# Sums of taps in four tiles of 32 tokens instead of two of 64, all four in one PSUM tile of four banks

## The chip, the cores and the metric

The kernel runs on one core of one Trainium2 chip. A core has five engines with a queue of instructions each: TensorE (PE, matrix products, with its weight loads shown apart as PEld), VectorE (DVE), ScalarE (ACT), GpSimd (POOL) and SyncE (SP). They meet through semaphores. TensorE writes its products to PSUM, a memory of 128 partitions by eight banks of 512 fp32 values each. Nothing else here writes it, and ACT copies its content to SBUF. The metric is the time of one execution on the device, in microseconds (us), and lower is better.

## The reference: a dynamic convolution and a maxout layer

The first half takes `x` (8 batches, 4160 tokens, 192 features) and `weight_gen` (8 heads, 7 taps for each token):

```python
w = np.exp(weight_gen - max); w = w / (np.sum(w, axis=-1, keepdims=True) + 1e-09)
x_pad = np.concatenate([zeros(B, 6, D), x], axis=1)
out = np.einsum('bshk,bskhg->bshg', w, x_unf)   # x_unf: seven neighbouring tokens
```

So each token becomes a weighted sum of itself and the six tokens before it, with weights of its own for each of 8 heads of 24 features. The second half is applied to each of the 33280 tokens:

```python
h1 = x @ w1; h2 = x @ w2          # 192 -> 1024
g = np.maximum(h1, h2)
out = g @ w_out                   # 1024 -> 192
```

## The kernel before: tiling, stages and the order of work

Tokens lie on 128 partitions, 260 consecutive ones ("columns") on each. The columns are worked through in batches of 16 and in units of 4 columns (the first eight units, which make up the first two batches) or 8 columns (the others).

For each unit DVE multiplies `x` by the weights, all seven taps at once, into `m_t` (`mul`, L192); the weights come from ACT (`en_t`, L177). The seven taps are then added and the result is transposed, so that features lie on partitions, as the products that follow need it. In the later units DVE does the additions (`adds`, L208 to L217) and a DMA transposes. In units 0 to 7 TensorE does both (`sum_transpose`, L249): it loads a piece of `m_t` as weights and multiplies by the identity, and the taps add up in PSUM. Before the change a piece is 64 partitions by 128 columns of `m_t`, and 64 columns of the identity move through it. For each of 6 pieces and each tap there are two such matmuls, one on either half of the partitions, that write two different banks: 84 in a unit (48 in unit 5, where four taps are left after an addition on DVE). ACT then copies the sum to `yt` (L265).

The maxout is written as `w_out` applied to `h1 + relu(h2 - h1)`. The difference of the two weights is `wd`, and `hid_tile` (L309) multiplies `yt` by it. ACT's relu (L319) brings the product to SBUF as `rd_t`. The part of `h1` is one product with `w10`, the product of `w1` and `w_out`, computed once at the start: `w1_transposed` (L617), ACT's copies to `w1t` (L689), `w10_product` (L671) and `w10_copies` (L680, L682). Results are collected in PSUM as `op_ps`: `out_first` writes the `w10` part (L361) and one half of the hidden features (L349), and `out_second` the other half. Between these two ACT passes a signal on (`relay`, L382), since the halves meet in one bank. ACT's `evac` (L405) copies the results to `o_t`, and SyncE stores them.

The order of instructions of each engine is that of the Python code (`manual_schedule`). The code of the start stands out line by line. After it, `hidden(g, ...)` (L470) issues one group of tiles at a time: all hidden tiles of the group but the last, `out_first`, relus, the last hidden tile, its relu, `out_second`, `evac`, and then whatever the table `early` adds for that group. Groups 4 to 7 have two hidden tiles each, and `early` puts `sum_transpose(4)` to `sum_transpose(7)` behind their `evac`. From group 8 on there are three tiles and `later_ps` has divided PSUM anew; units of 8 columns come through DVE and the DMA from there.

PSUM in the first stage has two pools of two buffers of two banks each. Pool "h" holds hidden products. Pool "o" holds, by turns, the sums of `sum_transpose` (`yps`), the transposed `w1` (`tp`), the product `pw` and the results `op_ps`. A new tile waits until the reader of the tile before the last is done with that buffer.

Of the kernel before, what the change touches and what calls it, by code (L numbers as in the profile page):

```python
# [9 lines left out]
FP32 = mybir.dt.float32  # L10
BF16 = mybir.dt.bfloat16
# [6 lines left out]
def _sub(base: bass.AP, off: int, dims):  # L18
    ap = [list(base.ap[0])] + [[int(s), int(c)] for s, c in dims]
    return dataclasses.replace(base, offset=base.offset + off, ap=ap)  # L20
# [3 lines left out]
def kernel(  # L24
# [9 lines left out]
    nc = tc.nc  # L34
# [4 lines left out]
    P = 128  # L39
# [25 lines left out]
    for b, (c0, n) in enumerate(BATCHES):  # L65
# [19 lines left out]
    pyt = work.enter_context(tc.tile_pool(name="pyt", bufs=6))  # L85
    prd = work.enter_context(tc.tile_pool(name="prd", bufs=7))
    first_ps = work.enter_context(ExitStack())
    ps = {k: first_ps.enter_context(tc.tile_pool(name="pps_" + k, bufs=2, space=bass.MemoryType.PSUM))
          for k in ("h", "o")}

    def later_ps():

# [8 lines left out]
    m_t = pm.tile([P, K * 16 * D], BF16, name="m_t")  # L101
# [141 lines left out]
    def half(j):  # L243
        return slice(64 * j, 64 * j + 64)
# [4 lines left out]
    def sum_transpose(u, taps=range(K)):  # L249

        b, o, n = UNITS[u]
        assert n == 4
        yps = ps["r" if "r" in ps else "o"].tile([P, 1024], FP32, name="yps", tag="op")
        for k in range(6):
            for t in taps:
                for r in range(2):
                    at = (K * o + t * n) * D + k * P
                    nc.tensor.matmul(  # L258
                        yps[:, r * 512 + k * 64:r * 512 + (k + 1) * 64],
                        lhsT=m_t[half(r), at:at + P], rhs=ident[half(r), half(r)],  # L260
                        start=(k == 0 and t == taps[0]), stop=(t == taps[-1]),
                        skip_group_check=True,
                    )
        yt = pyt.tile([P, 8 // 2 * 3 * P], BF16, name="yt", tag="yt")
        yt_of[u] = nc.scalar.copy(out=_sub(yt, 0, [[64, 2], [P, 6], [1, 64]]),  # L265
                                  in_=_sub(yps, 0, [[512, 2], [64, 6], [1, 64]]))
        yt_ts[u] = yt


    relu_of, yt_of, w10_of = {}, {}, []  # L270
# [168 lines left out]
    for g in range(3, len(GROUPS)):  # L439
        most = 4 if g == 3 else 2 if GROUPS[g][1] == 2 or len(OUTS[-1]) == 4 else 4  # L440
        n = min(most, ready[g] - c)
# [21 lines left out]
    def out_room(now, tag=None):  # L463
        tag = tag or ("r" if "r" in ps else "o")
        w, name = {"ab": (2048, "ab"), "c": (1024, "c")}.get(tag, (1024, "op"))
        tile_ = ps[tag].tile([P, w], FP32, name="op_ps", tag=name)
        for c in now:
            op_at[c // 2] = tile_, (c - now[0]) // 2 * D

    def hidden(g, now=(), between=lambda: None, beside=lambda: None, ahead=lambda: None):  # L470


        t0, n = GROUPS[g]
        rd = room(g)
        for t in range(t0, t0 + n - 1):
            hid_tile(t)
        if now:
            out_room(now, "ab" if n == 1 and "ab" in ps else None)
            last = out_first(now)
        if len(now) > 2:  # L480
            relu(rd, t0, n - 1)
        else:
            for t in range(t0, t0 + n - 1):
                relu(rd, t, 1)
        if now:
            go = relay(last)
        hid_tile(t0 + n - 1)
        if len(now) > 2:
            beside()
        relu(rd, t0 + n - 1, 1)  # L490
        ahead()
        if now:
            out_second(now, go)
            evac(now[0] // 2, len(now) // 2)
        between()
        if len(now) <= 2:
            beside()

    def rest_of_results(c):

        parts = [p for p in (c[:4], c[4:-2], c[-2:]) if p]
        assert max(map(len, parts)) <= 4
        go = []
        for i, now in enumerate(parts):
            out_room(now, ("r", "ab", "c")[i])
            go.append(relay(out_first(now)))
            if i:
                out_second(parts[i - 1], go[i - 1])
                evac(parts[i - 1][0] // 2, len(parts[i - 1]) // 2)
        out_second(parts[-1], go[-1])  # L510
        evac(parts[-1][0] // 2, len(parts[-1]) // 2)
# [6 lines left out]
    ident = consts.tile([P, P], BF16, name="ident")  # L518
# [9 lines left out]
    with tc.tile_pool(name="pstage", bufs=1) as pstage:  # L528
# [7 lines left out]
        for p0, p1 in ((1, 16), (16, P)):  # L536
            nc.sync.dma_start(  # L537
                out=xs[p0:p1, 0:PAD * D],
                in_=bass.AP(tensor=x.tensor, offset=(p0 * CPP - PAD) * D,
                            ap=[[CPP * D, p1 - p0], [1, PAD * D]]),  # L540
# [20 lines left out]
        for wi, wsrc in enumerate((moe_w1, moe_w2)):  # L561
            for h in range(2):
                nc.sync.dma_start(  # L563
                    out=ws["T", wi][half(h), :],
                    in_=bass.AP(tensor=wsrc.tensor, offset=P * F + h * HF, ap=[[F, 64], [1, HF]]),
# [20 lines left out]
        for o in (0, 4, 8, 12):  # L586
            weights(0, o)
        nc.vector.tensor_copy(out=xb_ts[0][:, PAD * D:(PAD + 4) * D],
                              in_=xs[:, PAD * D:(PAD + 4) * D])
# [19 lines left out]

        def w1_transposed():  # L610

            tp = ps["o"].tile([P, 1024], FP32, name="tp", tag="op")[:, :].bitcast(BF16)
            for at, kind, nr in ((0, "E", P), (P, "T", 64)):
                for fi in range(FCH):
                    o = fi // 4 * 1024 + fi % 4 * D
                    rows, c = (slice(0, P), fi) if kind == "E" else (half(fi // 4), fi % 4)
                    nc.tensor.matmul(  # L617
                        tp[:, o + at:o + at + nr],
                        lhsT=w1[kind][rows, c * P:(c + 1) * P],
                        rhs=ident[rows, rows], is_transpose=True, skip_group_check=True,  # L620
                    )
            return tp
# [3 lines left out]
        def keep_warm(times):  # L626
# [11 lines left out]
            out=wo[:, :].rearrange("p (f d) -> p f d", d=D),  # L638
            in_=bass.AP(tensor=moe_w_out.tensor, offset=0, ap=[[D, P], [P * D, FCH], [1, D]]),
        )  # L640

        sum_transpose(0)
        keep_warm(8)
        mul(0, 4)
# [10 lines left out]
        relu(rd, 1, 1)  # L655
        w_diff(1, nc.vector.tensor_copy)
        sum_transpose(1)
        red(1)
        mul(0, 8)
        hidden(1)  # L660
        ln(1)
        shift(1)
        mul(0, 12)
        tp = w1_transposed()

        def w10_product():

            pw = ps["o"].tile([P, 1024], FP32, name="pw", tag="op")
            for at, c0 in ((0, 0), (512, 64)):
                for fi in range(FCH):  # L670
                    nc.tensor.matmul(  # L671
                        pw[:, at:at + D], lhsT=w1t[:, fi * D + c0:fi * D + c0 + P],
                        rhs=wo[:, fi * D:(fi + 1) * D],
                        start=(fi == 0), stop=(fi == FCH - 1), skip_group_check=True,
                    )
            return pw
# [13 lines left out]
        weights(1, 0)  # L690
        mul(1, 0)
        sum_transpose(2)
        rd = room(3)
        for t in (6, 7):
            hid_tile(t)
        pw = w10_product()
        relu(rd, 6, 1)
        behind(relu_of[6], load_x(1, 8, 8))
# [175 lines left out]
    def steps(g, tiles):  # L874
# [3 lines left out]
        for t in tiles:  # L878
            extra(t)

    out_room(OUTS[3])
    go = relay(out_first(OUTS[3]))
    out_second(OUTS[3], go)
# [51 lines left out]
```

## Time and profile before

| what | value |
|---|---|
| median of 3 runs | 410.88 us (410.36 to 411.26) |
| the profiled execution | 410.26 us |
| its span, first to last instruction | 408.5 us |
| TensorE busy | 399.1 us, 7422 matmuls |
| VectorE busy | 377.5 us |
| ScalarE busy | 357.0 us |
| GpSimd busy | 76.3 us |
| sum matmuls (L258) | 636, from 12.4 to 48.7 us, 0.190 us from start to end of one |
| copies to `yt` (L265) | 8, 0.79 to 0.88 us each |
| mean granted TensorE clock | 0.998 |

The profile shows one execution. The span lacks what lies before the first and after the last instruction, 1.8 us here. Matmuls overlap, so that the time from one start to the next, and not the length of one, tells what a matmul costs in a row of them. A group such as "x84" in a list by time has the start of the first and the length to the end of the last. Words in brackets tell how long the engine was idle before and what released it.

### The profile page before, as it was taken

What the parts mean: (1) busy time and instruction counts of PE and PEld (TensorE: products, weight loads), DVE (VectorE), ACT (ScalarE), POOL (GpSimd) and SP (SyncE); (2) the same over time, 40 slices, a digit from 0 to 9 for tenths busy, and PEclk for the clock granted to TensorE, in tenths of its full rate; (3) what the DMA queues carried; (4) which work ended last, traced back from release to release, by engine and by line L of the source; (5) the groups of instructions that cost most, each with busy time, mean ns of one, the idle gap of its engine ahead of it and who ended that gap; (6) DMA issues with size and microseconds to landing.
All of it is one profiled execution on the core that took longest, in us unless ns stands there. A gap on an engine that the chain in (4) does not pass through costs nothing.

```text
span 408.5 us, 16193 instructions
## 1 busy us (share of the span) xinstructions
PE 399.1 (98%) x7422; PEld 317.4 (78%) x7422; DVE 377.5 (92%) x227; ACT 357.0 (87%) x424; POOL 76.3 (19%) x102
## 2 busy tenths in 40 slices
PE   7899999999999999999999999999999999999995
PEld 2689989777777877777777778777777877787795
DVE  5999999999999999999999999999999999999500
ACT  5899899999899998898998999998999889988872
POOL 0311012122222112122210122221122222110000
PEclk9999999999999999999999999999999999999999
DMA  8958397856657764974776588479557646964423
GB/s 238 228 127 219 73 195 164 184 141 169 156 111 237 164 147 109 239 200 74 237 197 98 118 239 202 72 236 196 108 120 229 168 80 221 159 125 130 126 76 124
DMA packets 62820, 65.72 MB, mean 161 GB/s; under 512 B 47743, under 2 KB 51711, under 8 KB 62750
## 3 DMA queue, kind: packets, MB, share of 16 engines
q1 hardware_dynamic: 54334, 40.54, 37.0%
q0 software_dynamic: 8272, 24.04, 29.4%
q8 instruction: 58, 0.95, 0.9%
q14 instruction: 12, 0.10, 0.1%
q10 hardware_dynamic: 144, 0.10, 0.1%
HBM read 35.96 MB, written 25.56 MB: 151 GB/s over the span
## 4 chain that ended last, share of the span: by engine, by line
PE 91%; ACT 5%; DMA 2%; SPq 1%; issue 1%; ACTq 0%
PE op_ps L349 41%; PE hd L309 39%; PE op_ps L361 8%; ACT rd_t L319 2%; DMA ws1T<-in_moe_w_dram 2%; PE hdp L309 1%; PE yps L258 1%; ACT yt L265 1%; SPq L563 1%; ACT w1t L689 0%; ACT e_t L137 0%; ACT en_t L177 0%; SPq L555 0%; SPq L537 0%; ACT wd L605 0%
## 5 line engine op out<-in xcount | busy, mean ns | idle before, releaser
L319 ACT ACTIVATE rd_t<-hd 128x1024 bf16<-128x1024 f32 (+1 forms) x206 | 234.7, 1188 | 27.5 <-PE hd L309 26.3
L349 PE MATMUL op_ps<-wo,rd_t 64*128 64x192 bf16 x4160 | 211.4, 243 | 0.1
L349 PEld LDWEIGHTS <-rd_t 64*128 64x128 bf16 x4160 | 181.7, 94 | 15.7 <-ACTq L382 0.3
L309 PE MATMUL hd<-yt,wd 64*128 64x512 bf16 (+1 forms) x1584 | 188.0, 360 | 0.7 <-issue 0.6
L192 DVE TENSOR_TENSOR m_t<-xb_t,en_t 128x10752 bf16<-128x10752 bf16 (+1 forms) x37 | 187.4, 5069 | 0.4 <-ACT en_t L177 0.3
L309 PEld LDWEIGHTS <-wd 64*128 64x128 bf16 x1776 | 94.3, 94 | 42.9 <-issue 2.3
L234 POOL CAST gate<-yt 128x1 f32<-128x1 bf16 x29 | 40.8, 1405 | 261.0 <-DMA yt<-y_t 261.0
L208 DVE TENSOR_TENSOR m_t<-m_t 128x4608 bf16<-128x4608 bf16 (+1 forms) x30 | 74.1, 2469 | 0.1
L405 ACT COPY o_t<-op_ps 128x384 f32<-128x384 f32 (+1 forms) x99 | 57.3, 589 | 12.8 <-PE op_ps L349 12.8
L361 PE MATMUL op_ps<-w,yt 64*128 64x192 bf16 x780 | 55.9, 243 | 0.2 <-ACT w L682 0.2
L361 PEld LDWEIGHTS <-yt 64*128 64x128 bf16 x780 | 38.6, 94 | 16.5 <-issue 1.1
L214 DVE TENSOR_TENSOR m_t<-m_t 128x3072 bf16<-128x3072 bf16 (+1 forms) x29 | 49.9, 1721 | 0.1
L177 ACT ACTIVATE en_t<-wg_t 128x896 bf16<-128x896 f32 (+2 forms) x45 | 35.8, 821 | 0.0
L217 DVE TENSOR_TENSOR y_t<-m_t 128x1536 bf16<-128x1536 bf16 (+1 forms) x29 | 27.3, 940 | 0.5
L116 POOL DMA_DIRECT2D xb_t<-in_x_dram x33 | 17.7, 537 | 31.9 <-ACT rd_t L319 19.9
L166 DVE TENSOR_TENSOR wg_t<-wg_t,ln_t 128x280 f32<-128x280 f32 (+5 forms) x46 | 22.0, 480 | 0.0
L137 ACT ACTIVATE e_t<-wg_t 128x896 f32<-128x896 f32 (+2 forms) x18 | 16.1, 901 | 2.6 <-DMA wg_t<-in_weight_gen_dram 2.6
L155 DVE TENSOR_REDUCE s_rest<-e_t 128x64 f32<-128x448 f32 (+2 forms) x27 | 16.2, 601 | 0.5 <-ACT e_t L137 0.5
L319 ACT ACTIVATE rd_t<-hdp 128x1024 bf16<-128x1024 f32 x16 | 16.2, 1061 | 0.4 <-PE hdp L309 0.4
L629 PE MATMUL warm<-ident 128*128 128x512 bf16 x38 | 10.9, 455 | 2.7 <-DVE ident L576 2.7
L309 PE MATMUL hdp<-yt,wd 64*128 64x256 bf16 x192 | 13.1, 269 | 0.3 <-issue 0.2
L258 PEld LDWEIGHTS <-m_t 64*128 64x128 bf16 x636 | 10.2, 95 | 2.7 <-DVE m_t L192 2.3
(54 smaller groups left out, 76.2 us busy)
## 6 DMA issues: line engine op xcount, KB each, us to landing
out_dram<-o_t SPq DMA_DIRECT2D x22, 768.0 KB, 4.6
xb_t<-in_x_dram POOLq DMA_DIRECT2D x30, 384.0 KB, 5.2
out_dram<-o_t SPq DMA_DIRECT2D x20, 384.0 KB, 3.1
wg_t<-in_weight_gen_dram POOLq DMA_DIRECT2D x14, 448.0 KB, 5.5
xb_t<-xb_t POOLq DMA_DIRECT2D x16, 288.0 KB, 5.3
wg_t<-in_weight_gen_dram SPq DMA_DIRECT2D x2, 448.0 KB, 4.6
xs<-in_x_dram SPq DMA_DIRECT2D x2, 384.0 KB, 6.3
xb_t<-in_x_dram POOLq DMA_DIRECT2D x3, 192.0 KB, 5.1
```

The lines of the kernel that those rows point to most:

```text
L166: nc.vector.tensor_tensor(out=w_t, in0=w_t, in1=_sub(s_ts[b], hs.start, [[1, hs.stop - hs.start], [0, K]]), op=ALU.subtract)
L177: nc.scalar.activation(out=_sub(en_ts[b], (o * WGC + j * N * K) * 2, [[2 * N, K], [2, N], [1, 2]]), in_=_sub(wg_ts[b], (o * H + j * N) * K ...
L192: return nc.vector.tensor_tensor(out=m_out, in0=x_in, in1=_sub(en_ts[b], o * WGC * 2, [[2, K * n * H], [0, G // 2], [1, 2]]), op=ALU.mult,)
L208: nc.vector.tensor_tensor(out=taps(0, 1, 3), in0=taps(0, 1, 3), in1=taps(3, 1, 3), op=ALU.add)
L214: nc.vector.tensor_tensor(out=taps(0, 2, 2), in0=taps(0, 2, 2), in1=taps(1, 5, 2), op=ALU.add)
L217: nc.vector.tensor_tensor(out=_sub(y_ts[b], o * D, [[64, 2], [P, 3 * w // 2], [1, 64]]), in0=taps(0, 1, 1), in1=taps(2, 1, 1), op=ALU.add,)
L234: nc.gpsimd.tensor_copy(out=gate, in_=yt[:, 0:1])
L309: nc.tensor.matmul(hid_out(t, f, j), lhsT=wd_at(j, s, f // 4, f % 4 * P, P), rhs=_sub(yt_ts[u][half(j), :], (s + j) % 3 * P, [[3 * P, w // ...
L319: relu_of[t0] = nc.scalar.activation(out=rd[:, k * 1024:(k + n) * 1024], in_=hd[:, at:at + n * 1024], func=AF.Relu)
L349: return nc.tensor.matmul(op_out(c), lhsT=rd[half(r), k * 1024 + at:k * 1024 + at + P], rhs=wo[half(r), f * D:(f + 1) * D], start=False, s ...
L361: nc.tensor.matmul(op_out(c + j), lhsT=yt_ts[u][half(j), (3 * i + (s + j) % 3) * P:(3 * i + (s + j) % 3 + 1) * P], rhs=w10[half(j), s * D: ...
L405: nc.scalar.copy(out=_sub(o, c % 24 * D, [[D, len(qs)], [h * D, 2], [1, D]]), in_=_sub(tile_, at + (qs[0] - p) * D, [[D, len(qs)], [512, 2 ...
```

## The change: four row tiles, four banks, halves by turns

The pool "o" has one buffer. One tile `four` of 2048 fp32 values (four banks) is taken from it once. `sum_transpose` now splits the tokens of a piece in four tiles of 32 partitions. Each is multiplied by the 32x32 block of the identity on the same partitions and writes a bank of its own, so a unit has 168 matmuls of 32 moving columns (96 in unit 5) and its copy reads four banks. All other users of the pool in the first stage (`tp`, `pw`, `op_ps`) get one half of `four` from the new function `two_banks`, the two halves by turns. Lines behind the new function move down by 6.

```diff
--- before.py
+++ after.py
@@ -85,8 +85,14 @@
     pyt = work.enter_context(tc.tile_pool(name="pyt", bufs=6))
     prd = work.enter_context(tc.tile_pool(name="prd", bufs=7))
     first_ps = work.enter_context(ExitStack())
-    ps = {k: first_ps.enter_context(tc.tile_pool(name="pps_" + k, bufs=2, space=bass.MemoryType.PSUM))
-          for k in ("h", "o")}
+    ps = {k: first_ps.enter_context(tc.tile_pool(name="pps_" + k, bufs=n, space=bass.MemoryType.PSUM))
+          for k, n in (("h", 2), ("o", 1))}
+
+    four = [ps["o"].tile([P, 2048], FP32, name="four", tag="op"), 0]
+
+    def two_banks():
+        four[1] ^= 1024
+        return four[0][:, four[1]:four[1] + 1024]
 
     def later_ps():
 
@@ -250,20 +256,20 @@
 
         b, o, n = UNITS[u]
         assert n == 4
-        yps = ps["r" if "r" in ps else "o"].tile([P, 1024], FP32, name="yps", tag="op")
         for k in range(6):
             for t in taps:
-                for r in range(2):
+                for r in range(4):
                     at = (K * o + t * n) * D + k * P
+                    rows = slice(32 * r, 32 * r + 32)
                     nc.tensor.matmul(
-                        yps[:, r * 512 + k * 64:r * 512 + (k + 1) * 64],
-                        lhsT=m_t[half(r), at:at + P], rhs=ident[half(r), half(r)],
+                        four[0][:, r * 512 + k * 32:r * 512 + (k + 1) * 32],
+                        lhsT=m_t[rows, at:at + P], rhs=ident[rows, rows],
                         start=(k == 0 and t == taps[0]), stop=(t == taps[-1]),
                         skip_group_check=True,
                     )
         yt = pyt.tile([P, 8 // 2 * 3 * P], BF16, name="yt", tag="yt")
-        yt_of[u] = nc.scalar.copy(out=_sub(yt, 0, [[64, 2], [P, 6], [1, 64]]),
-                                  in_=_sub(yps, 0, [[512, 2], [64, 6], [1, 64]]))
+        yt_of[u] = nc.scalar.copy(out=_sub(yt, 0, [[32, 4], [P, 6], [1, 32]]),
+                                  in_=_sub(four[0], 0, [[512, 4], [32, 6], [1, 32]]))
         yt_ts[u] = yt
 
 
@@ -463,7 +469,7 @@
     def out_room(now, tag=None):
         tag = tag or ("r" if "r" in ps else "o")
         w, name = {"ab": (2048, "ab"), "c": (1024, "c")}.get(tag, (1024, "op"))
-        tile_ = ps[tag].tile([P, w], FP32, name="op_ps", tag=name)
+        tile_ = two_banks() if tag == "o" else ps[tag].tile([P, w], FP32, name="op_ps", tag=name)
         for c in now:
             op_at[c // 2] = tile_, (c - now[0]) // 2 * D
 
@@ -609,7 +615,7 @@
 
         def w1_transposed():
 
-            tp = ps["o"].tile([P, 1024], FP32, name="tp", tag="op")[:, :].bitcast(BF16)
+            tp = two_banks().bitcast(BF16)
             for at, kind, nr in ((0, "E", P), (P, "T", 64)):
                 for fi in range(FCH):
                     o = fi // 4 * 1024 + fi % 4 * D
@@ -665,7 +671,7 @@
 
         def w10_product():
 
-            pw = ps["o"].tile([P, 1024], FP32, name="pw", tag="op")
+            pw = two_banks()
             for at, c0 in ((0, 0), (512, 64)):
                 for fi in range(FCH):
                     nc.tensor.matmul(
```

## The prediction

> **What bounds the kernel now.** I read the shares of busy time first, then the chain that ended last, then stretches of the span, then the instructions in order of time around the changed lines on TensorE (PE) and ScalarE (ACT).
>
> ```profile
> PE 399.1 (98%) x7422; PEld 317.4 (78%) x7422; DVE 377.5 (92%) x227; ACT 357.0 (87%) x424; POOL 76.3 (19%) x102
> ...
> PE 91%; ACT 5%; DMA 2%; SPq 1%; issue 1%; ACTq 0%
> ```
>
> The chain is TensorE's. Two stretches, us from the start:
>
> ```profile
> 31.00:49.00 18.00, 17.72 (x584) 16.82 (x580) 18.00 (x10) 16.93 (x28) 2.14 (x4) 1.00 0.54 146
> 49.00:390.00 341.00, 340.28 (x5967) 268.74 (x5965) 333.67 (x193) 306.66 (x344) 68.30 (x83) 1.00 0.69 162
> ```
>
> From 49 to 390 us PE is busy 340.28 of 341.00 us. Its shape there is always the same: sixteen 192-column matmuls in 0.66 us, 41.2 ns each. Nothing later can give back what is lost before 49 us. So the forecast is the time by which the first 24-matmul group of the steady part (at 48.70 us) moves. The changed code is all before that. PE, start and length:
>
> ```profile
> 22.99 1.40 PE L258 MATMUL yps<-ident,m_t 64*128 64x64 bf16 x84 [0.18 <-DVE m_t L192]
> 24.22 1.47 PE L309 MATMUL hdp<-yt,wd 64*128 64x256 bf16 x24
> 25.63 1.50 PE L671 MATMUL pw<-wo,w1t 128*128 128x192 bf16 x16
> 27.05 1.40 PE L258 MATMUL yps<-ident,m_t 64*128 64x64 bf16 x84
> 28.62 0.42 PE L361 MATMUL op_ps<-w,yt 64*128 64x192 bf16 x6 [0.16 <-ACT w L682]
> ...
> 34.26 0.82 PE L349 MATMUL op_ps<-wo,rd_t 64*128 64x192 bf16 x16
> 34.92 1.39 PE L258 MATMUL yps<-ident,m_t 64*128 64x64 bf16 x84
> 36.15 0.82 PE L309 MATMUL hdp<-yt,wd 64*128 64x256 bf16 x12
> 36.80 0.41 PE L361 MATMUL op_ps<-w,yt 64*128 64x192 bf16 x6
> ```
>
> And ACT over the same time:
>
> ```profile
> 23.78 1.55 ACT L689 COPY w1t<-tp 128x768 bf16<-128x768 bf16 x2
> ...
> 27.93 0.64 ACT L682 CAST w<-pw 64x192 bf16<-64x192 f32 x2
> ...
> 30.95 0.79 ACT L265 CAST yt<-yps 128x768 bf16<-128x768 f32 x1
> ...
> 36.19 0.46 ACT L405 COPY o_t<-op_ps 128x384 f32<-128x384 f32 x1
> 36.55 0.81 ACT L265 CAST yt<-yps 128x768 bf16<-128x768 f32 x1
> ```
>
> To see: PE runs ahead of ACT. The block of unit 2 starts at 22.99, before ACT copies out `w1t` (25.33); that of unit 3 at 27.05, before the copies of `w10` are done (28.57); that of unit 4 at 34.92, 1.3 us before ACT empties (36.19) what PE finished just before it. It can, because it has a PSUM buffer of its own.
>
> **The change, part by part.**
>
> *The sum matmuls.* 84 a block become 168 (48 become 96 in unit 5), half as wide. Now a pair on the two row halves takes 29.2 ns (84 in 1.23 us); the matmuls of other widths fit columns/2.4 + 2.5 ns a pair (192: 82.4, 256: 109), and the two of a pair start 3 ns apart. Four row groups side by side at 32 columns would give 15.9 ns for each four; if the weight load, still 128 columns, sets the pace, four take 29.2 ns as two do now. No row is nearer to one end, so I take the middle, 22.6: a block of 42 fours is 0.95 us, 0.28 less than now. [...]
>
> *Changes of row tiling.* Now the block and its neighbours all use 64 rows (only the small weight products use 128). With 32 rows PE changes shape before and after each block. From the last 128x128 transposing matmul of L617 at 20.61 to the first 64-row one at 20.765 the trace has 0.152 us where 0.056 is usual, and from L671 to L258 0.178 where 0.082 is usual: 0.096 each. I take 0.1 us, bounds 0 and 0.2: some 0.2 us a block, so the block itself gains 0.1 us at most.
>
> *The waits.* Sums now write all four banks, so each block waits until ACT has emptied both halves, and whatever small product comes next waits for the block's own copy to `yt`. I walk through PE's and ACT's order with the durations above (ACT's from start to start: relu 0.91, `yt` 0.68, `en_t` 0.30 each, 0.93 if long, `e_t` 0.85, a two-column result 0.36; 0.05 us from an end to the start that it releases). Before -> after:
>
> - Units 0 and 1: free. Unit 0's block ends at 13.79 and ACT takes it at 14.88; unit 1's ends at 18.97, taken at 19.28. The transposed `w1` now waits for unit 1's copy (20.09) and started at 20.21. With the cover gone, at most 1.2 us for each.
> - Unit 2's block waits for the second `w1t` copy, 25.33: 22.99 -> 25.4. Queued behind it on PE: the hidden tiles 24.22 -> 26.4, the product `pw` 25.63 -> 27.8, ending 29.4 with its latency. ACT waits for them too (`yt`, relu), so its last `w10` copy ends 28.57 -> 30.5.
> - Unit 3's block waits for that copy: 27.05 -> 30.6.
> - The first results (L361) waited only for `w10`, 28.62. Now they wait for unit 3's `yt`, which on ACT stands behind two `en_t`, a relu and `e_t`: 30.5 + 0.6 + 0.9 + 0.85 + 0.8 = 33.65; start 33.7. Their second half was held until 30.71 by ACT's relay; now it follows at once (44 matmuls, 1.8 us, 0.3 for the relay, 32 more, 1.3). The hidden tiles of the next group: 32.04 -> 37.1, +5.1.
> - Then a ring closes between PE and ACT: results evacuated (0.46), block (0.1 + 0.95 + 0.17 latency + 0.05), `yt` (0.8 + 0.05), 22 result matmuls (0.91), hidden tile (0.66 + 0.26), its relu (0.91), then again the evacuation, which ACT takes only after the relu: 5.3 us a turn with the small gaps, 4.9 for the shorter unit 5. Now a turn is 4.10, 3.65 and 4.44 us (34.92, 39.02, 42.67, 47.11). In the first, `en_t` and `ln` (0.8) also stand before the evacuation. Blocks: 34.92 -> 42.3, 39.02 -> 47.6, 42.67 -> 52.5, 47.11 -> 57.8.
> - The steady part: 48.70 -> 58.9, +10.2. The same walk on the old order gives 47.97, not 48.70: it lacks 0.73 us of gaps that the trace puts to issue (0.16 at 44.71, 0.12 and 0.3 within the last block). If those stay the difference is 10.9, if PE's new waits cover them 10.2. I take 10.6.
>
> *More instructions.* 1,272 rows more on PE, while the page has 58 packets of 16 KB of them for 14,844. The gaps just named, and one of 0.57 at 54.77, come where nothing else is waited for. Bounds: 1.0 less (they vanish) to 0.28 a block, 2.2 more. I take 0.
>
> *Copies to `yt`, two_banks, the pool.* The copy has the same 128x768 elements in runs of 32, not 64. L405's of 768 in runs of 192 takes 0.80, L265's 0.81, so run length shows no price: 0, bounds 0.05 either way a copy. The alternation gives the small products the halves that two buffers gave them, and as many banks. DVE's multiplications wait for the blocks that read `m_t`, by the walk 8 to 9 us later at 55 us, less than PE: free, as long as PE is later still. Loads that a relu releases move with ACT, likewise inside PE's delay.
>
> **Sum.** The profiled execution took 410.26 us, 408.5 of span and 1.8 around it; the median of the runs is 410.88, 0.6 above. 410.26 + 10.6 = 420.9; on the median 421.5. Fours at 15.9 or 29.2 ns: 1.2 less or more. Tiling changes at 0 or 0.2: 0.3 less, 0.6 more. With instructions: 418.5 to 425.5 if all ends add.
>
> **The rivals.**
>
> - *Row groups in turn.* If four 32-row matmuls cost two of today's pairs (58.4 ns), blocks last 2.45 us: 1.5 more in five and a half blocks, 8.4, and 1 from unit 1, whose cover goes: 431. For it: 168 weight loads of 128 columns. Against: today's pairs start 3 ns apart.
> - *The ring is looser.* ACT's relays run ahead of its queue (the result matmuls started at 30.71 while its `yt` copy was only at 30.95); if its other work slid out of the ring, only the +5.1 of the start stays: 416. Against: the evacuation reads what PE has just written, and the block must wait for that.
> - *Clock.* The first eleven `warm` matmuls stand 0.427 us apart, those after 7.65 us 0.216: a start at half pace that cost 2.3 us. If PE's new waits (2.1 us the longest, ahead of 33.7) bring that back once or twice, 424 to 427. Against: waits of up to 0.69 us now do no such thing. [...]
> - *Faster.* No new wait bites, since ACT gets ahead, and fours take 15.9 ns. On PE's chain are units 4 to 7: 3 x 0.56 + 0.32 saved, 8 x 0.1 of tiling changes paid: 1.2 less, 409.7. It decides only where ACT has emptied the results before PE's next instruction: 36.19 would have to be 34.92, though the last matmul into these banks starts at 34.84.
>
> **How the numbers follow.** Forecast 421.5, chance 0.80 (own range 418.5 to 425.5); row groups in turn 0.06; looser ring 0.05; clock 0.05; faster 0.03; 0.01 for no change. What a measurement can tell from no change is 0.2%, 0.8 us. Range 418.5 to 426.5, which leaves out the first, second and fourth rivals. Faster 0.03, same 0.01, slower 0.96.
>
> **What would show it.** Sum blocks near 25.4, 30.6, 42.3, 47.6, 52.5 and 57.8; PE idle before them with ACT's `w1t`, `w10` and o_t copies as releasers, and idle before the first result matmuls (L361) with `yt` as releaser; block length 0.67 to 1.23 us; the first 24-matmul hidden group near 59; from there the same pace as before. Wrong if blocks start straight after the result matmuls, if they last 2.4 us, or if matmuls after a wait stand twice as far apart.

## The result: 8.6% slower, more than three times the loss that was forecast

The changed kernel takes 446.31 us (median of 4 runs, 444.49 to 447.6), the kernel before 410.69 us beside it. The ratio is 1.0863, 95% interval 1.082 to 1.0905. The profiled execution took 447.6 us, with a span of 445.7 us. The forecast was 421.5 us, with a range of 418.5 to 426.5. The direction was right; the size was not.

The page of the changed kernel: busy time; TensorE (PE) and its granted clock in forty slices; the instruction queue among the DMA queues; the chain that ended last.

```profile
PE 411.8 (92%) x8058; PEld 326.4 (73%) x8058; DVE 378.1 (85%) x227; ACT 358.5 (80%) x424; POOL 74.5 (17%) x102
...
PE   7566867699999999999999999999999999999996
...
PEclk9976768899999999999999999999999999999999
...
q8 instruction: 63, 1.03, 0.9%
...
PE 88%; ACT 4%; issue 4%; DMA 3%; DVE 1%; SPq 0%; ACTq 0%; DVEq 0%
```

All of the loss lies in the first eight slices (89 us). There PE is busy for 50 to 89% of a slice and, which nothing before had shown, its mean granted clock falls to between 0.6 and 0.9 of full speed in slices three to eight. "issue", time in which an engine waits for nothing that the profile shows, has gone from 1% to 4% of the span. Later nothing has changed. Stretches of the changed kernel (us, then busy us of PE, its weight loads, DVE, ACT, POOL, then the clock):

```profile
31.00:49.00 18.00, 11.48 (x420) 10.05 (x419) 9.73 (x6) 7.82 (x15) 1.61 (x3) 0.67 0.36 93
49.00:88.00 39.00, 26.90 (x912) 22.92 (x910) 21.64 (x12) 17.04 (x24) 1.61 (x3) 0.81 0.34 76
88.00:390.00 302.00, 301.85 (x5308) 238.55 (x5304) 295.22 (x163) 275.56 (x311) 62.76 (x76) 1.00 0.67 162
```

The steady part, whose first group of 24 hidden matmuls was to show the whole difference, starts at 85.30 us where it started at 48.70: 36.6 us later, and the span is 37.2 us longer (445.7 - 408.5). So that was the right place to look. PE in order of time in the changed kernel, with start, length and count; idle time before and its releaser in brackets:

```profile
2.65 8.51 PE L635 MATMUL warm<-ident 128*128 128x512 bf16 x30 [2.65 <-DVE ident L582]
12.52 1.52 PE L264 MATMUL four<-ident,m_t 32*128 32x32 bf16 x168 [1.35 <-DVE m_t L198]
13.97 1.90 PE L635 MATMUL warm<-ident 128*128 128x512 bf16 x8
15.86 1.49 PE L315 MATMUL hdp<-yt,wd 64*128 64x256 bf16 x24
17.54 1.13 PE L264 MATMUL four<-ident,m_t 32*128 32x32 bf16 x121 [0.19 <-DVE m_t L198]
23.30 0.55 PE L264 MATMUL four<-ident,m_t 32*128 32x32 bf16 x47 [4.63 <-issue]
23.78 2.74 PE L315 MATMUL hdp<-yt,wd 64*128 64x256 bf16 x24
26.46 0.83 PE L623 MATMUL four<-ident,w1E 128*128 128x128 bf16 x8
27.22 0.30 PE L623 MATMUL four<-ident,w1T 64*128 64x64 bf16 x8
27.35 1.48 PE L315 MATMUL hdp<-yt,wd 64*128 64x256 bf16 x24
31.60 1.33 PE L264 MATMUL four<-ident,m_t 32*128 32x32 bf16 x145 [2.77 <-ACT w1t L695]
35.97 0.35 PE L264 MATMUL four<-ident,m_t 32*128 32x32 bf16 x23 [3.04 <-issue]
36.25 2.74 PE L315 MATMUL hdp<-yt,wd 64*128 64x256 bf16 x24
```

Three things are to be seen. The wait of unit 2's block for `w1t` is there (2.77 us), as forecast. But two blocks of sums stop in their middle, for 4.63 and 3.04 us, with no semaphore. And behind each of these stops the same 24 hidden matmuls take 2.74 us, where they take 1.49 at 15.86: half the pace.

The stops obey a count. Up to the first, PE has issued 30 + 168 + 8 + 24 + 121 = 351 matmuls; up to the second 351 + 47 + 24 + 16 + 24 + 145 = 607. Three more follow, at 1119, 1503 and 1759. All five are 95 plus a multiple of 128. A matmul stands twice on the page, as PE and as PEld (x8058 each), which I count as two rows of code, so that 128 of them are 256 rows. The page's instruction queue, q8, has 63 packets (1.03 MB, 16 KB each) where there were 58, and 8058 and 7422 matmuls are 62.95 and 57.98 times 256 rows. That these packets are PE's code, 256 rows in each, I conclude from this agreement; no line of the page says it. The gaps before the change, which the prediction put to "issue" without more, stand at 991, 1119 and 1247: the same count. These lines are of the kernel before, its instruction queue and the longest of the gaps:

```profile
q8 instruction: 58, 0.95, 0.9%
...
54.50 0.27 PE L309 MATMUL hd<-yt,wd 64*128 64x256 bf16 x1
55.34 0.83 PE L309 MATMUL hd<-yt,wd 64*128 64x256 bf16 x11 [0.57 <-issue]
```

So it looks as if PE had no code. I call this theory C. The rival, W, was that the new waits on PSUM are the cause, and the stops in the blocks are waits of a kind that the profile does not show. The stops sum up to 15.1 us in the list of waits (us in all, times, longest):

```profile
PE four L264 <- issue: 15.1, 5, 4.6
```

### The profile page after: what moved, and what is told of

The parts are those of the page before. It is cut to its first block, busy times and chain, and to the rows that moved or that the text cites. A ratio compares the mean times of both kernels' runs of the same rounds, so it can differ in the third digit from the quotient of the medians.

```text
span 445.7 us, 17464 instructions
## 1 busy us (share of the span) xinstructions
PE 411.8 (92%) x8058; PEld 326.4 (73%) x8058; DVE 378.1 (85%) x227; ACT 358.5 (80%) x424; POOL 74.5 (17%) x102
## 3 DMA queue, kind: packets, MB, share of 16 engines
q8 instruction: 63, 1.03, 0.9%
## 4 chain that ended last, share of the span: by engine, by line
PE 88%; ACT 4%; issue 4%; DMA 3%; DVE 1%; SPq 0%; ACTq 0%; DVEq 0%
PE op_ps L355 36%; PE hd L315 36%; PE op_ps L367 7%; PE hdp L315 3%; DMA xs<-in_x_dram 3%; PE four L264 2%; ACT rd_t L325 2%; PE four L355 2%; DVE m_t L198 1%; PE four L367 1%; ACT o_t L411 1%; PE four L677 1%; ACT yt L271 0%; ACT w1t L695 0%; ACT en_t L183 0%
## 5 line engine op out<-in xcount | busy, mean ns | idle before, releaser
L355 PE MATMUL op_ps<-wo,rd_t 64*128 64x192 bf16 x3968 | 200.6, 243 | 0.0
L355 PEld LDWEIGHTS <-rd_t 64*128 64x128 bf16 x4160 | 183.6, 95 | 16.2 <-ACTq L388 0.5
L315 PEld LDWEIGHTS <-wd 64*128 64x128 bf16 x1776 | 95.5, 97 | 43.8 <-issue 0.7
L240 POOL CAST gate<-yt 128x1 f32<-128x1 bf16 x29 | 39.2, 1350 | 263.0 <-DMA yt<-y_t 263.0
L411 ACT COPY o_t<-op_ps 128x384 f32<-128x384 f32 (+1 forms) x94 | 54.4, 590 | 12.7 <-PE op_ps L355 12.7
L367 PE MATMUL op_ps<-w,yt 64*128 64x192 bf16 x744 | 53.2, 244 | 0.0
L264 PE MATMUL four<-ident,m_t 32*128 32x32 bf16 x1272 | 12.3, 178 | 24.7 <-issue 15.1
L264 PEld LDWEIGHTS <-m_t 32*128 32x128 bf16 x1272 | 11.6, 91 | 26.8 <-issue 24.5
L271 ACT CAST yt<-four 128x768 bf16<-128x768 f32 x8 | 6.4, 798 | 20.5 <-PE four L264 20.3
```

What stands on the lines that cost most here:

```text
L240: nc.gpsimd.tensor_copy(out=gate, in_=yt[:, 0:1])
L264: nc.tensor.matmul(four[0][:, r * 512 + k * 32:r * 512 + (k + 1) * 32], lhsT=m_t[rows, at:at + P], rhs=ident[rows, rows], start=(k == 0 an ...
L315: nc.tensor.matmul(hid_out(t, f, j), lhsT=wd_at(j, s, f // 4, f % 4 * P, P), rhs=_sub(yt_ts[u][half(j), :], (s + j) % 3 * P, [[3 * P, w // ...
L355: return nc.tensor.matmul(op_out(c), lhsT=rd[half(r), k * 1024 + at:k * 1024 + at + P], rhs=wo[half(r), f * D:(f + 1) * D], start=False, s ...
L367: nc.tensor.matmul(op_out(c + j), lhsT=yt_ts[u][half(j), (3 * i + (s + j) % 3) * P:(3 * i + (s + j) % 3 + 1) * P], rhs=w10[half(j), s * D: ...
L411: nc.scalar.copy(out=_sub(o, c % 24 * D, [[D, len(qs)], [h * D, 2], [1, D]]), in_=_sub(tile_, at + (qs[0] - p) * D, [[D, len(qs)], [512, 2 ...
```

## The experiments

### The waits alone

The tile `four` and all its waits stay; the sums are again pairs of 64 partitions, 84 in a unit, written to the first and the third of the four banks.

```diff
-                for r in range(4):
+                for r in range(2):
...
-                    rows = slice(32 * r, 32 * r + 32)
+                    rows = half(r)
                     nc.tensor.matmul(
-                        four[0][:, r * 512 + k * 32:r * 512 + (k + 1) * 32],
+                        four[0][:, r * 1024 + k * 64:r * 1024 + (k + 1) * 64],
```

> The changed kernel's one PSUM tile and all its waits, but with the sums as before: pairs of 64 partitions, 84 matmuls a unit, into the first and the third of the four banks. Theory C (PE runs out of instructions: they come in pieces of 256 rows, 128 matmuls, and a piece that is used up in less than some 3 us is followed by a stop): no more code than before, so no stop above 1 us without a semaphore; what is left is the walk of waits, 58.7 us for the block of unit 7 and 12 us in all, 420 to 426. Theory W (the new waits themselves stop PE, the stops within blocks are waits that the profile does not show, and the half clock follows from them): 435 or more.

Measured: 421.64 us, ratio 1.0296 (1.0241 to 1.035). PE in order of time in this run:

```profile
25.41 1.40 PE L264 MATMUL four<-ident,m_t 64*128 64x64 bf16 x84 [2.58 <-ACT w1t L695]
...
30.76 1.40 PE L264 MATMUL four<-ident,m_t 64*128 64x64 bf16 x84 [1.22 <-ACT w L688]
33.94 0.42 PE L367 MATMUL four<-w,yt 64*128 64x192 bf16 x6 [1.77 <-ACT yt L271]
...
42.54 1.40 PE L264 MATMUL four<-ident,m_t 64*128 64x64 bf16 x84 [1.60 <-ACT o_t L411]
...
58.54 1.40 PE L264 MATMUL four<-ident,m_t 64*128 64x64 bf16 x84 [0.82 <-ACT o_t L411]
59.76 1.49 PE L315 MATMUL hd<-yt,wd 64*128 64x256 bf16 x24
```

Each releaser in brackets is the one that the prediction's walk named, and the blocks stand at 25.4, 30.8, 42.5 and 58.5 us, where the walk had 25.4, 30.6, 42.3 and 57.8 (with shorter blocks). There is no stop without a semaphore above 0.25 us, and the granted clock is 1.00. So the waits cost 59.76 - 48.70 = 11.1 us, and W falls: the stops in the blocks don't come from the waits. For the half clock this is less certain. The execution shown took 420.53 us and another 420.01 us, both at a mean granted clock of 1.00; the other two had 0.995 and 0.991 and took 422.76 and 423.52 us (the kernel before, beside it, has 0.995 to 1.00). The waits by themselves can thus cost some of the clock, though no more than 3.5 us in this run.

### The code alone

The kernel before, with its own pools and waits. Each sum matmul is split in two of 32 columns, on the same 64 partitions.

```diff
-                for r in range(2):
+                for h, r in ((0, 0), (0, 1), (1, 0), (1, 1)):
...
-                        yps[:, r * 512 + k * 64:r * 512 + (k + 1) * 64],
-                        lhsT=m_t[half(r), at:at + P], rhs=ident[half(r), half(r)],
+                        yps[:, to:to + 32], lhsT=m_t[half(r), at:at + P],
+                        rhs=ident[half(r), 64 * r + 32 * h:64 * r + 32 * h + 32],
```

> The kernel before, its pools and waits, with each sum matmul split in two of 32 columns on the same 64 partitions: 168 a unit, no 32-row tiles. Blocks last 2.1 us instead of 1.23 at 25 ns a pair. Theory C: stops of 1.5 to 5 us where the count of matmuls is 95 + a multiple of 128 and that falls in a block, and half clock behind them, 420 to 435. Theory W: only the longer blocks, 0.87 us for each of units 4, 6 and 7, 0.5 for unit 5: 413.5 to 415.

Measured: 431.62 us, ratio 1.0508 (1.0444 to 1.0572). No wait was added. The list by time of this run:

```profile
17.83 1.68 PE L259 MATMUL yps<-ident,m_t 64*128 64x32 bf16 x121
23.03 0.80 PE L259 MATMUL yps<-ident,m_t 64*128 64x32 bf16 x47 [3.52 <-issue]
23.67 2.72 PE L310 MATMUL hdp<-yt,wd 64*128 64x256 bf16 x24
...
29.32 1.98 PE L259 MATMUL yps<-ident,m_t 64*128 64x32 bf16 x145
32.30 0.45 PE L259 MATMUL yps<-ident,m_t 64*128 64x32 bf16 x23 [1.01 <-issue]
```

The breaks fall after 121 and 145 matmuls, exactly where they fall in the changed kernel, though neither the row tiles nor the banks nor the waits are the same: only the count is. Stops of 0.9 to 3.5 us come at 351, 607, 863, 1119, 1503 and 1759. They sum up to 10.5 us of idle time. The clock is at half for 13.7 us before the steady part, which starts 21.5 us late (70.23). Doubling the code of the blocks thus costs 22 us here with pools and waits as they were, of which the longer blocks (168 at 12.5 ns, 2.1 us instead of 1.2) explain less than 7.

### The same code, moved

The changed kernel, with 76 warm matmuls of 16 columns ahead of the long ones, of which 26 stay. The blocks begin 72 matmuls later in the count.

```diff
-        keep_warm(30)
+        for _ in range(76):
+            nc.tensor.matmul(warm[:, 0:16], lhsT=ident, rhs=ident[:, 0:16],
+                             start=True, stop=True, skip_group_check=True)
+        keep_warm(26)
```

> The changed kernel with 76 warm matmuls of 16 columns put ahead of the first ones and 26 instead of 30 of the long ones, 72 matmuls more, so that the piece ends fall elsewhere: only one in most blocks, where there were two in units 2, 4, 6 and 7. Theory C: stops within blocks gone or under 1.5 us each, 422 to 430. Theory W: 444 to 448, as the changed kernel.

Measured: 438.04 us, ratio 1.0712 (1.0651 to 1.0773), with 432.95 us in the profiled execution. This is between the two expectations. The stops went where C says: none is left within a block of sums (unit 1's and unit 2's, which broke at 121 and 145, are now whole), and all that remain stand at 95 plus a multiple of 128 (479, 1247, 1375, 1631, 1887). By time, in this run:

```profile
18.34 1.52 PE L264 MATMUL four<-ident,m_t 32*128 32x32 bf16 x168 [0.95 <-DVE m_t L198]
...
23.63 1.86 PE L315 MATMUL hdp<-yt,wd 64*128 64x256 bf16 x15 [3.12 <-issue]
...
31.86 1.53 PE L264 MATMUL four<-ident,m_t 32*128 32x32 bf16 x168 [2.50 <-ACT w1t L698]
```

But they did not vanish: the first is merely moved behind a block, and the five are still 5.1 us of idle time instead of 15.1. The rest of the spread is the clock: the mean granted clock was 0.986 in the profiled execution and 0.968 to 0.972 in the three timed ones, which took 437 to 441 us.

### The waits with little code

The changed kernel, with three of the seven taps (two in unit 5); the other taps are left out of the sum, so the time is that of less work. A block has 72 matmuls.

```diff
-    def sum_transpose(u, taps=range(K)):
+    def sum_transpose(u, taps=range(3)):
...
-        5: (lambda: (weights(2, 0), sum_transpose(5, LEFT)), none),
+        5: (lambda: (weights(2, 0), sum_transpose(5, range(2))), none),
```

> The changed kernel with three of the seven taps summed on PE (two in unit 5), the rest left out: 72 matmuls of 32 partitions a unit, fewer than the 84 before; waits, banks and changes of row tiling as changed. Theory C: no stop within blocks, the walk gives 57.1 us instead of 48 for the steady part, 418 to 424. Theory W: 432 or more.

Measured: 425.16 us, ratio 1.036 (1.032 to 1.0401): a little above C's 418 to 424, far from W's 432. No block stops, and the steady part starts at 62.88 us, not at the walk's 57.1. The difference is the clock, at half for 13.7 us in three stretches from 26.6 us on, by which the matmuls there were about 5.6 us later. The first stretch begins here:

```profile
25.75 0.72 PE L264 MATMUL four<-ident,m_t 32*128 32x32 bf16 x72 [2.58 <-ACT w1t L695]
26.40 2.55 PE L315 MATMUL hdp<-yt,wd 64*128 64x256 bf16 x24
```

This kernel's waits are nearly those of the run with the waits alone, whose profiled execution kept its clock; the longest is 2.58 us in both. What differs is how much PE does between them (72 small matmuls in 0.72 us, not 84 in 1.40) and where in time they fall. The point on the clock, below, comes back to this.

### One stop, to price the clock

The kernel before, with eight or fourteen short copies on ACT in group 24, in the steady part. The group's first result matmul waits for the last copy.

```diff
+        if g == 24:
+            for _ in range(8):
+                last_copy = nc.scalar.copy(out=o_last, in_=wo[:, 0:2 * D])
+            stop.append(last_copy)
```

> The kernel before with one stop of PE put into group 24, in the steady part: eight copies of 384 elements on ACT (about 0.4 us each) ahead of the group's relus, and the group's first result matmul waits for the last. No code added on PE. PE stops for about 2 us, as in the changed kernel's new waits. [...] If any stop of 2 us costs the clock: half pace behind it, 5 us or more.

> The same with fourteen copies: a stop of 4.5 to 5 us, as long as the longest within a sum block of the changed kernel (4.8 us). If a stop of this length brings half the clock for one or two stretches of 3.4 us: the stop and 1.7 to 3.4 us more, 6.5 to 8.5 us in all, and matmuls twice as far apart behind it. If the clock needs something else to fall: 4.5 to 5.5 us.

Measured: 416.36 us, ratio 1.017 (1.0146 to 1.0194), and 420.06 us, ratio 1.0263 (1.0233 to 1.0294). The copies took 0.54 us each rather than 0.4, so the stops were longer than planned. With eight copies:

```profile
119.55 0.42 PE L362 MATMUL op_ps<-w,yt 64*128 64x192 bf16 x6 [4.93 <-ACT o_last L482]
119.81 1.29 PE L350 MATMUL op_ps<-wo,rd_t 64*128 64x192 bf16 x16
```

With fourteen:

```profile
123.10 0.66 PE L362 MATMUL op_ps<-w,yt 64*128 64x192 bf16 x6 [8.19 <-ACT o_last L482]
123.56 1.49 PE L350 MATMUL op_ps<-wo,rd_t 64*128 64x192 bf16 x16
```

Sixteen result matmuls take 0.82 to 0.84 us at the full clock, 1.49 at half. A stop of 4.93 us was followed by 3.4 us of half clock, and the kernel lost 6.8 us: the stop, and 1.7 us for half of that stretch. A stop of 8.19 us had 10.2 us of half clock, half of it within the stop, and cost 10.5 us, the stop and 2.3. So the stop of 4.93 us cost a third more than it lasted. A stop of about 2 us, for which this was also meant, did not come about here; the run with the waits alone has one of 2.58 us without a loss of clock, the run with three taps one of 2.58 us with a loss.

### The code before, moved

The kernel before with 40, 88, 16 and 112 matmuls more in the same manner (44 short and 26 long warm ones, 96 and 22, 18 and 28, 120 and 22).

> The kernel before with 44 short warm matmuls ahead and 26 long ones instead of 30, 40 matmuls more, so that its pieces of code end elsewhere. Theory C: its three stops of 0.3, 0.3 and 0.7 us (matmuls 991, 1119 and 1247) go from there, and others stand only at 95 + a multiple of 128 of its own count; time between 1.3 us less and 1.5 more: 408.5 to 411.5. If the stops belong to the places in the work: they stay at 44.4, 48.3 and 54.5 us.

> As before with 96 short and 22 long warm matmuls, 88 more. Theory C: stops only at 95 + a multiple of 128 of its own count, 408.5 to 411.5. If the stops belong to the places in the work: they stay where they were.

> The kernel before with 18 short and 28 long warm matmuls, 16 more matmuls: the ends of its pieces of code fall 16 matmuls earlier in the work, still close to those that stop for 0.3, 0.3 and 0.7 us. Theory C: stops at 95 + a multiple of 128 of its own count, 0.5 to 3 us together; 409 to 413. If only the amount of code mattered, not where its pieces end: 409.5.

> The same with 120 short and 22 long warm matmuls, 112 more, which puts the ends 16 matmuls later in the work than in the kernel before. Theory C: 0.5 to 3 us of stops, 408.5 to 413, and faster than the kernel before if they come to less than its 1.3 us. If only the amount mattered: 409.5.

Measured: 414.14 us, ratio 1.0099 (1.0064 to 1.0134); 412.69 us, 1.008 (1.0059 to 1.0101); 409.83 us, 0.9996 (0.9974 to 1.0017); 410.36 us, 1.0011 (0.9992 to 1.0029). All stops over 0.25 us without a semaphore in the first part of the four traces stand at 95 plus a multiple of 128 of the kernel's own count, among them these two with 40 more, which break a block of sums and a hidden tile:

```profile
40.84 0.34 PE L258 MATMUL yps<-ident,m_t 64*128 64x64 bf16 x11 [1.26 <-issue]
...
54.49 1.15 PE L309 MATMUL hd<-yt,wd 64*128 64x256 bf16 x17 [0.94 <-issue]
```

The stops belong to the count, then, and not to a place in the work. With 40 and 88 more the kernel before is up to 1% slower, past what I had allowed for. Moving the ends by 16 either way changed nothing that can be measured, and no position beat the kernel before. How much of that 1% the stops make is only partly shown. With 40 more they grow from 0.9 to 3.3 us, and PE's last matmul comes 2.8 us later. With 88 more they are 1.9 us, yet in the profiled execution, the fastest of its six, PE ends no later than before; with 112 more they are 1.7 us, and the time is the same.

## Why the prediction was wrong, point by point

- **PE bounds, and nothing after 49 us gives anything back: right.** The steady part is 36.6 us late, the span 37.2 us longer.
- **The waits: right, place by place.** By themselves they cost 11.1 us and 421.64 us in all, where the whole forecast was 421.5. That the totals agree to 0.1 us is partly luck: the forecast also had shorter blocks and changes of tiling, and its ring of 5.3 and 4.9 us a turn took 5.5 and 5.0.
- **More instructions, taken at 0 and bounded at 2.2 us: this is the step that failed.** I priced it with the gap of 0.28 us that the kernel before has in one block. By theory C that gap is what is left of a delivery when PE is just too fast for it, not the price of one that is wholly uncovered. The right reading was a rate. The twelve traces have 36 stops of over 0.2 us before 90 us, and their records of the instruction queue show the same order at each. PE passes one of the counts of 95 + 128 n; 0.2 to 5.6 us later a packet starts; it takes 0.9 to 1.4 us (1.9 to 4.1 in four cases); and PE, which has meanwhile stopped at the next count, resumes 1.0 to 1.6 us after the packet's end. At the five stops of the changed kernel these times are 0.85 to 4.35, 0.93 to 0.98 and 1.28 to 1.45 us. So PE had taken at least 2.6 us from passing one count to going on behind the next wherever it stopped, in the changed kernel 3.2 us or more (56.7 to 59.9, 71.3 to 74.5), and 6.6 around the first stop. In steady work 128 matmuls take over 5 us (41.2 ns each at the least), and but for the gap of 0.57 us at 54.77 no stop is seen there. In a block of sums they take about 1 us (1.04 from 56.69 to 57.73 in the changed kernel), and a block of 168 meets one count always and two often. The five stops sum up to 15.1 us.
- **The clock, a rival at 0.05, "once or twice": it happened, six times, and I had its cause too narrow.** I looked at the length of the new waits, 2.1 us at most (2.77 measured). But the stops for code add to them, up to 4.6 us. The clock was at half for 34.1 us before 90 us; taking half of each distance between matmul starts in those stretches, about 12 us were lost so, 10.6 of them before the steady part starts. The length of one wait does not tell when: the run with three taps lost the clock three times with no idle time above 2.58 us, while the changed kernel's wait of 2.77 us (28.84 to 31.60) lies in a stretch at full clock, which goes on to 33.77.
- **What the length of a wait leaves out.** In the clock records of the twelve traces the granted clock keeps one value for whole steps of 3.41 us: stretches of half clock within the work last 3.41, 6.83 or 10.24 us. Wherever it fell before 130 us, PE had been busy for only 0.2 to 2.1 us of the last step at full clock (in the changed kernel 1.77, 1.33, 2.13, 1.82, 1.40 and 0.23 us). Behind steps with 1.4 to 2.1 us it sometimes fell and sometimes held (there it held behind 2.06 and 1.89); in these traces it never fell behind one with more. In the run with three taps the wait of 2.58 us lies within one step (23.23 to 26.64, PE busy for 0.89 us); in the run with the waits alone it is shared by two, with 2.17 and 1.98 us of work. How much idle time a step happens to catch is then partly chance, and it may be why executions of one kernel differ in their clock.
- **The sum: 11.1 for the waits, 15.1 for the code and 10.6 for the clock up to the steady part make 36.8, where 36.6 are seen.** That it comes so close is partly luck: the sum leaves out the longer blocks, and in the changed kernel the waits for ACT are 10.3 us, against 10.8 in the run with the waits alone.
- **The sum matmuls: four row groups do run side by side (33.3 ns for four, where two of the pairs of before in turn are 58.4), but the block became longer, outside my bounds.** A block of 168 takes 1.35 us from its first start to its last (1.52 less the 0.17 of the last one), where 84 took 1.21. The first eight fours come every 25 ns; from there on they come every 33.3 ns, 8.3 ns for each matmul with its weight load, at full clock. With 64 rows and 32 columns a pair takes 25 ns throughout, 12.5 ns a matmul. So the 33.3 ns is not set by columns, and the saving of 0.28 us a block that I counted was a loss of 0.13.
- **Changes of row tiling, 0.1 us: right.** From the last sum to the first hidden matmul behind unit 5's block there are 0.111 us, against 0.010 in the run with the waits alone and 0.026 before, where both have 64 rows. The change into a block can't be read, since a wait stands before every one.
- **Row groups in turn, a looser ring, faster: none of them came.**
- **Slips in the working that changed nothing.** The gaps listed for 0.73 us on the old order come to 0.58, and the 0.12 and 0.3 in the last block seem to be one stop, that of matmul 1119, told twice. The lower end of the sum is 421.5 less 1.2, 0.3 and 1.0, which is 419.0 and not 418.5.

## What to carry to other kernels

Before splitting matmuls into smaller ones, count rows of code per microsecond, and look in the trace for "issue" gaps at a fixed count: here PE stopped, with no semaphore to wait for, where it had done 128 matmuls before it could go on, 2.6 to 7.8 us after the last count; by theory C that is when its code came. The gaps of at most 0.57 us before the change said nothing of what became of them when the code of the blocks doubled, stops of 2.01 to 4.63 us. And price a stop with the clock: the one of 4.93 us in dense work cost itself and about 1.7 us more, and in the run with three taps waits of at most 2.58 us close together went with about 5.6 us.

## What the runs showed of the hardware that I had not expected

- PE stops at fixed counts: in all twelve traces, each stop of PE over 0.2 us without a semaphore before 90 us stands at 95 + 128 n matmuls. From one count to the packet's start it takes 0.85 to 4.35 us in the changed kernel; its two longest stops (4.63 and 3.36 us) came while the DMA engines were busy almost without a break (a share of 1.07 from 16.73 to 23.30 us and of 1.05 from 80.54 to 85.15), the two of 2.01 us while they had a busy share of 0.24 and 0.02 (56.69 to 59.93 and 71.31 to 74.52). That their load makes the delay longer is a guess from these few.
- Matmuls of 32 rows and 32 columns, each with a weight load of its own, settle at 8.3 ns each in the changed kernel's first block, after 32 that take 6.2.
- 40 or 88 matmuls more at the start, in otherwise idle time, made the kernel before slower by 1.0 and 0.8%, 16 or 112 more did not. The stops at the counts are part of it (3.3 us with 40 more, where there were 0.9); that they are all of it isn't shown.
- Half clock came after a stop of 4.93 us in dense work, but also after 2.58 us where PE had little to do around it: what tells them apart in these traces is PE's work in steps of 3.41 us (0.89 us in the step with that wait), not the length of a wait. Behind 1.4 to 2.1 us of work in a step the clock went either way; whether there is a fixed bound, and what counts as work, is not shown.
